# Top-k attention and two MoE layers on one core: half-chunk weight tiles, plain 32-bit scores for one batch, a guard on GpSimd, and new planner constants

## The chip, the cores and the metric

One Trainium2 chip, one core. The metric is the device time of one execution in microseconds; the time before is the median of three runs.

## The reference

Attention over 4 batches, 8 heads, 576 rows and a head size of 64. Of each row of scores only the 32 largest count; the rest are set to -1e9 ahead of the softmax. The attended rows, 2304 x 512, go through two dense layers (called MoE in the code):

```
scores = scale * q @ k.T;  kth = 32nd largest of the row
scores = where(scores >= kth, scores, -1e9)
attn   = exp(scores - max) / (sum + 1e-9);   x = attn @ v
x = (relu(x @ w_in) ** 2) @ w_out                    # 512 -> 2048 -> 512
x = max(x @ w1, x @ w2, x @ w3) @ w_out2             # 512 -> 768 -> 512
```

The weights come as 64-bit floats. All products must be good to about single precision.

## The kernel before, in words

The program is built by a planner that is part of it (class Plan, lines 85 to 243). Every operation is entered with its engine, a cost in ns (c_act, c_dve, c_pool and c_mm, lines 246 to 259), a priority, the buffers it reads and writes, and in some cases a slack: that many ns are added to the time at which the planner thinks it ready. Plan.run plays the program through once with these costs, hands out buffers by their number (nbufs, line 273), and so fixes the order in which each engine's instructions stand. On the chip each engine, and SP as the only queue that issues DMAs, then works through its list in that order and waits at each instruction for what it needs. Constants of the model: DBW, DL0, DL1 and DTR (line 35) are the DMA's bytes per ns, two latencies and the time of one transpose.

**Attention.** The work is cut into eight units (line 323): a batch's full 128-row tiles, three, one or three at a time, and a remainder of 64 rows of two heads. Each unit runs four times, once for each pair of heads p (attend, line 404). prep_k and prep_q (lines 354 and 390) load k and q already laid out, twice over in 128 partitions; ScalarE rounds all of it to the reduced 32-bit format of TensorE (lines 359 and 399), and GpSimd replaces it by the difference: in k for the lower 64 partitions, in q as a second plane. So one product over 128 partitions with the plane of high parts, and one with the plane of low parts, make the score (lines 494 to 504): two matmuls of 288 columns for each half of a score tile, four in the remainder. ScalarE scales them into s (line 429). Then VectorE takes the top 32 of 576 in four rounds of max (line 435) with three of match-replace between them (line 437); GpSimd makes a bias nb (line 439); ScalarE masks, takes exp and casts to 16 bits (lines 441 to 446); GpSimd makes the low 16-bit part; SP issues a DMA that transposes both parts (line 451); TensorE multiplies by v in nine small matmuls (line 462); ScalarE copies the result with its row sum into xs (line 465).

finish_x (line 506) divides by the row sum: VectorE adds a guard and doubles (line 508, slack 1000 ns), VectorE takes the reciprocal (line 510), GpSimd adds the two parts (line 515) and multiplies (line 516). TensorE transposes into x (lines 471, 486), ScalarE and VectorE split that into a high and a low part (lines 474, 476, 488, 490). There are 64 such divisions and 144 score tiles: 24, 12, 12 and 24 in the four units of the first two batches, and the same again.

**MoE.** Units 0; 1 and 2; 3; 4; 5 and 6; 7 feed six passes of 384 rows (moe, line 574). Each pass takes 28 weight chunks (8 of w_in, 8 of w_out, 9 of w1 to w3, 3 of w_out2), and each product is three matmuls: high x high, high x low, low x high (line 599). weights (line 535) brings a chunk as a tile wt of 2 x 1024 columns, four buffers. In the first pass a chunk is converted from 64-bit floats in two halves: SP loads the raw words into one of three slots (line 550), ScalarE forms the exponent part (line 557, through the helper line 308), VectorE shifts and merges (lines 559 and 561), ScalarE rounds to the high part (line 563), GpSimd subtracts for the low part (line 565, through the helper line 305), and SP stores the whole chunk to DRAM (line 567). The other five passes load chunks from there (line 540). A chunk's matmuls wait for the whole tile.

Of the kernel before, what the change touches and what calls it, by code (L numbers as in the profile page):

```python
# [23 lines left out]
D = 64  # L24
# [10 lines left out]
DBW, DL0, DL1, DTR = 360.0, 1280.0, 900.0, 1500.0  # L35
# [32 lines left out]
class Half:  # L68


    def __init__(self, bf, x):
        self.bf, self.x = bf, x

    def __getitem__(self, idx):
        return self.bf[(idx[0], self.x, *idx[1:])]

    def key(self, k):
        return self.bf, (self.x, k)
# [6 lines left out]
class Plan:  # L85
# [11 lines left out]
    def op(self, eng, ns, prio, reads, writes, fn, lat=0.0, slack=0.0):  # L97
        reads, writes = ([x[0].key(x[1]) if isinstance(x, tuple) and isinstance(x[0], Half) else x for x in y]
# [159 lines left out]
def c_mm(n):  # L258
    return max(n / 2.4 + 2.5, 107.0)
# [3 lines left out]
def kernel(ctx, tc, q, k, v, w_in, w_out, w1, w2, w3, w_out2, out):  # L263
# [9 lines left out]
    nbufs = {"ks": 1, "qs": 1, "vst": 2, "kt": 4, "qt": 1, "vt": 4, "vs": 1, "sm": 2, "sc": 2, "us": 6, "s": 6, "w": 2, "e": 3, "e16": 2,  # L273
             "et": 2, "mx": 4, "nb": 4, "rc": 4, "xs": 2, "xr": 2, "xg": 3, "xt": 3, "cv": 3,
             "hh": 6, "hl": 6, "r": 2, "m0": 1, "m1": 1, "ot": 2, "wt": 4,
# [64 lines left out]
    NRAW = 3  # L340
    wtile = buf("xt", [P, 2, KD, NW], F32R)
    work = [(wtile, x) for x in range(2 * KD * NW // 1024)]
    while len(work) < NRAW:
        t = const.tile([P, 2, KD, P], F32R, name=f"raw{len(work)}")
        work.append((keep(t), 0))
# [3 lines left out]
    kv = {}  # L349

# [39 lines left out]
    def prep_q(i, unit, p):  # L390
        b, tl, rem = unit[:3]
        w = len(tl) * 2 * P
        n = w + (3 * D if rem else 0)
        qs = buf("qs", [P, QW])
        ld(lambda: qs[:, 0:w], q[b, p, :, tl[0] * 2 * P:tl[0] * 2 * P + w], (qs, 0), P * w)
# [8 lines left out]
    def attend(i, unit, p):  # L404
# [10 lines left out]
        if g not in xt:  # L415
            t = buf("xt", [P, 2, KD, NW], F32R)
            xt[g] = Half(t, 0), Half(t, 1)
        xh, xl = xt[g]
        xg = buf("xg", [P, XW, P])
# [3 lines left out]
        for j, h in jobs:  # L423
            s = buf("s", [P, S])
            for f in range(2):
                ps = buf("b", [P, 512])
                cs = slice(f * HS, (f + 1) * HS)
                pe(A_S, c_mm(HS) * (2 if j >= 0 else 4), [kt, qt], [ps, (s, f)], scores(j, h, nt, qt, kt, ps, cs))
# [3 lines left out]
            for r in range(4):  # L432
# [3 lines left out]
                if r < 3:  # L436
                    dve(A_X, S, [src, (mx, r)], [w_], lambda src=src, mx=mx, m8=m8, w_=w_: nc.vector.match_replace(  # L437
                        out=w_[:], in_to_replace=mx[:, m8], in_values=src[:], imm_value=-3.0e38))
            gps(A_E, 1, [(mx, 0), (mx, 3)], [nb], lambda mx=mx, nb=nb: nc.gpsimd.tensor_scalar(  # L439
# [14 lines left out]
            for hh, c0, c1 in ([(0, 0, D), (1, D, P)] if j < 0 else [(h, 0, P)]):  # L454
# [9 lines left out]
                pe(A_E, 400.0, [et, vt], [ps, (xs, (max(j, 0) % 2, hh)), (xg, (j, hh))], av)  # L464
                act(A_X, VW, [ps], [(xs, (max(j, 0) % 2, hh))], lambda ps=ps, xs=xs, m=m, j=j, hh=hh: nc.scalar.copy(
                    xs[0:m, max(j, 0) % 2, hh, :], ps[0:m, 0:VW]))
            if j < 0:
# [19 lines left out]
        pe(A_S, 107.0 * nt, [xg], [ps, (xh, (p, col)), (xl, (p, col))], f)  # L487
        act(A_S, w, [ps, us], [(xh, (p, col))], lambda: nc.scalar.activation(
            xh[:, p, col:col + w], ps[:, 0:w], AF.Copy, scale=us[:]), ptr=1)
        dve(A_S, w, [ps, us, (xh, (p, col))], [(xl, (p, col))], lambda: nc.vector.scalar_tensor_tensor(  # L490
            xl[:, p, col:col + w], ps[:, 0:w], us[:], xh[:, p, col:col + w].bitcast(F32),
            op0=ALU.mult, op1=ALU.subtract), slack=SL / 2)

    def scores(j, h, nt, qt, kt, ps, cs):
        def run():
            if j >= 0:
                o = j * 2 * P + h * P
                seq = [(qt[:, x, o:o + P], kt[:, h, cs]) for x in range(2)]
# [34 lines left out]
    scratch = [keep(dr.tile([P, 2048], F32, name=f"wsc{n}")) for n in range(NCH)]  # L533

    def weights(g, n):
        src = chunk_src[n]
        a, f = src.shape[1], src.shape[2]
        wt = buf("wt", [P, 2, 1024], F32R)
        if g > 0:
            dma(W_, P * 8192, [scratch[n]], [wt], lambda: nc.sync.dma_start(  # L540
                wt[:].rearrange("p a b -> p (a b)").bitcast(F32), scratch[n][:]))
        else:
            for x in range(2):
                wk, off = raw = work[(2 * n + x) % len(work)]

                def part(u, wk=wk, off=off):
                    return wk[:].rearrange("p x a b -> p (x a b)").bitcast(U32)[
                        :, 1024 * off:1024 * off + 1024].rearrange("p (n u) -> p n u", u=2)[:, :, u]

                dma(W_, P * 4096, [], [raw], lambda x=x, wk=wk, off=off: nc.sync.dma_start(  # L550
                    wk[:].rearrange("p x a b -> p (x a b)").bitcast(U32)[
                        :, 1024 * off:1024 * off + 1024].rearrange("p (a f) -> p a f", f=f),
                    src[:, x * a // 2:(x + 1) * a // 2, :]))
                hi, lo = (wt, 2 * x), (wt, 2 * x + 1)
                cv = buf("cv", [P, 512], U32)
                words = lambda cv=cv: cv[:]
                act(C_M, 512, [raw], [cv], lambda part=part, cv=cv: prelu(
                    cv[:].bitcast(F32), part(1).bitcast(F32), -2.0 ** 32, scale=2.0 ** -112), psum=False)
                dve(C_D, 512, [cv], [cv], lambda cv=cv: nc.vector.tensor_scalar(  # L559
                    cv[:], cv[:], 3, None, op0=ALU.logical_shift_left), rate=0.5, slack=SL / 2)  # L560
                dve(C_D, 512, [raw, cv], [cv], lambda part=part, cv=cv: nc.vector.scalar_tensor_tensor(  # L561
                    cv[:], part(0), 29, cv[:], op0=ALU.logical_shift_right, op1=ALU.bitwise_or), rate=1.6)
# [193 lines left out]
```

## Time and profile before

| | us |
|---|---|
| median of 3 runs | 1109.63 (1108.77 to 1112.27) |
| profiled execution, its own time | 1109.87 |
| its span, first to last instruction | 1108.1 |
| mean granted TensorE clock in it | 0.912 |

| engine | busy us | share of the span |
|---|---|---|
| TensorE matmul | 962.6 | 87% |
| TensorE weight load | 892.5 | 81% |
| VectorE | 886.8 | 80% |
| ScalarE | 747.3 | 67% |
| GpSimd | 646.8 | 58% |

Busy time counts instructions in execution. A matmul's end is modelled, so the mean time of one matmul is longer than the distance from one to the next. A wait is put down to the engine and line that released it. In rows, PE is TensorE, PEld its weight loads, DVE VectorE, ACT ScalarE, POOL GpSimd, SP the queue that issues DMAs; L508 is line 508. "issue" is time in which an engine waited for nothing that the profile shows.

### The profile page before, as it was taken

The page shows a single profiled execution, that of the slowest core. Times are in us where ns is not written, and L with a number is a line of the kernel's source. Part 1 is how long each engine was busy: PE and PEld are TensorE (multiplying, and loading weights), DVE is VectorE, ACT ScalarE, POOL GpSimd, SP SyncE. Part 2 cuts the span into 40 slices and gives each one's busy share as a digit, 9 for nine tenths or more (in the row PEclk, how much of TensorE's full clock was granted, in tenths as well). Part 3 has the DMA queues.
Part 4 walks back from the last instruction along what each step waited for, and adds up shares of the span by engine and source line. Part 5 has one row for each costly group of instructions (what it writes and reads, how often), then busy time and mean ns, then how long its engine had stood idle before and what let it go on. Part 6 is the DMA issues. An engine that isn't in the chain of part 4 may idle for free.

```text
span 1108.1 us, 18444 instructions
## 1 busy us (share of the span) xinstructions
PE 962.6 (87%) x6116; PEld 892.5 (81%) x6116; DVE 886.8 (80%) x1856; ACT 747.3 (67%) x1572; POOL 646.8 (58%) x835
## 2 busy tenths in 40 slices
PE   3455527987878799999999999999999999999998
PEld 2344426876767689989899998899998999989997
DVE  7999999999999999899999999999999931100020
ACT  7776758887876777887888877978866753123321
POOL 5754568988887756665665768666655552112211
PEclk8556557998878899999999999999999999999999
DMA  8544595999899999999999999999999996776663
GB/s 290 138 93 68 119 300 142 311 261 285 275 287 303 279 328 325 270 293 277 291 265 271 278 280 265 251 273 251 247 273 267 268 279 248 249 257 254 262 243 140
DMA packets 221343, 278.56 MB, mean 251 GB/s; under 512 B 175680, under 2 KB 179776, under 8 KB 199744
## 3 DMA queue, kind: packets, MB, share of 16 engines
q1 hardware_dynamic: 221248, 277.39, 85.2%
q8 instruction: 48, 0.79, 0.3%
q14 instruction: 47, 0.39, 0.1%
HBM read 200.80 MB, written 34.08 MB: 212 GB/s over the span
## 4 chain that ended last, share of the span: by engine, by line
PE 49%; DVE 34%; DMA 6%; issue 4%; ACT 3%; POOL 3%; SPq 0%; POOLq 0%; ACTq 0%; DVEq 0%
PE a L599 32%; DVE mx L435 14%; DVE w L437 12%; PE b L599 10%; DMA et<-e 5%; PE b L503 3%; PE b L462 3%; DVE cv L561 3%; DVE cv L559 2%; DVE rc L508 1%; DMA xt<-in_moe_w_in_dram 1%; POOL hl L305 1%; POOL e L305 1%; PE b L486 0%; DVE m L650 0%
## 5 line engine op out<-in xcount | busy, mean ns | idle before, releaser
L435 DVE MAX8 mx<-w 128x8 f32<-128x576 f32 x432 | 312.0, 743 | 0.4
L305 POOL TENSOR_TENSOR e<-e,e 128x512 f16<-128x512 f32 (+1 forms) x288 | 215.1, 764 | 98.2 <-ACT e L446 64.8
L599 PE MATMUL a<-xt,wt 128*128 128x384 f32 x1296 | 249.8, 345 | 7.2 <-POOL wt L305 3.2
L599 PEld LDWEIGHTS a<-xt,wt 128*128 128x128 f32 x1296 | 228.6, 192 | 11.1 <-POOL wt L305 4.6
L599 PE MATMUL b<-xt,wt 128*128 128x384 f32 x1152 | 231.5, 344 | 0.4 <-DVE xt L490 0.4
L599 PE MATMUL a<-hh,wt 128*128 128x384 f32 x768 | 225.4, 346 | 0.1
L437 DVE MATCH_REPLACE8 w<-mx,w 128x576 f32<-128x576 f32 x288 | 212.1, 738 | 0.0
L599 PEld LDWEIGHTS b<-xt,wt 128*128 128x128 f32 x1152 | 203.4, 191 | 1.7 <-DVE xt L490 0.8
L503 PE MATMUL b<-kt,qt 128*128 128x288 f32 x640 | 139.0, 345 | 49.7 <-ACT s L429 16.4
L305 POOL TENSOR_TENSOR hl<-r,hh 128x384 fp32r<-128x384 f32 x96 | 99.5, 1036 | 140.8 <-ACT hh L625 133.8
L503 PEld LDWEIGHTS b<-kt,qt 128*128 128x128 f32 x640 | 114.5, 222 | 61.0 <-ACT s L429 20.4
L308 ACT ACTIVATE e<-s,mx 128x576 f32<-128x576 f32 x144 | 111.8, 778 | 58.4 <-DVE mx L435 49.9
L462 PEld LDWEIGHTS <-et 128*128 128x128 f16 (+1 forms) x1440 | 87.0, 110 | 75.7 <-DMA et<-e 45.3
L462 PE MATMUL b<-vt,et 128*128 128x129 f16 (+3 forms) x1440 | 103.2, 225 | 48.8 <-DMA et<-e 26.2
L599 PEld LDWEIGHTS a<-hh,wt 128*128 128x128 f32 x768 | 142.9, 190 | 1.0 <-ACT hh L625 0.4
L599 PE MATMUL a<-hl,wt 128*128 128x384 f32 x384 | 131.9, 344 | 11.6 <-POOL hl L305 11.4
L429 ACT ACTIVATE s<-b 128x288 f32<-128x288 f32 x288 | 107.3, 408 | 16.3 <-PE b L503 15.1
L443 ACT ACTIVATE e<-e,nb 128x576 f32<-128x576 f32 x144 | 111.7, 778 | 6.5 <-POOL nb L439 3.9
L435 DVE MAX8 mx<-s 128x8 f32<-128x576 f32 x144 | 106.2, 743 | 5.5 <-ACT e L308 5.5
L437 DVE MATCH_REPLACE8 w<-mx,s 128x576 f32<-128x576 f32 x144 | 106.2, 738 | 0.0
L446 ACT CAST e<-e 128x576 f16<-128x576 f32 x144 | 97.2, 676 | 10.1 <-DMA et<-e 9.7
L623 ACT ACTIVATE r<-b 128x384 f32<-128x384 f32 x96 | 46.9, 489 | 75.0 <-PE b L599 74.9
(60 smaller groups left out, 1257.4 us busy)
## 6 DMA issues: line engine op xcount, KB each, us to landing
wt<-wsc SPq DMA_DIRECT2D x140, 1024.0 KB, 5.5
wsc<-wt SPq DMA_DIRECT2D x28, 1024.0 KB, 5.9
xt<-in_moe_w_out_dram SPq DMA_DIRECT2D x22, 512.0 KB, 4.7
ks<-in_k_dram SPq DMA_DIRECT2D x16, 576.0 KB, 4.8
xt<-in_moe_w_dram SPq DMA_DIRECT2D x18, 512.0 KB, 4.8
xt<-in_moe_w_in_dram SPq DMA_DIRECT2D x16, 512.0 KB, 5.2
qs<-in_q_dram SPq DMA_DIRECT2D x16, 384.0 KB, 5.0
vst<-in_v_dram SPq DMA_DIRECT2D x16, 320.0 KB, 4.7
```

Of the source, the lines that this page charges most:

```text
L305: eng.tensor_tensor(out_ap, a, b, op=ALU.subtract)
L308: return nc.scalar.activation(out_ap, src, AF.Prelu, alpha=slope, **kw)
L429: act(A_S, HS, [ps], [(s, f)], lambda s=s, cs=cs, ps=ps: nc.scalar.activation(s[:, cs], ps[:, 0:HS], AF.Copy, scale=escale))
L435: dve(A_X, S, [src], [(mx, r)], lambda src=src, mx=mx, m8=m8: nc.vector.max(out=mx[:, m8], in_=src[:]))
L437: dve(A_X, S, [src, (mx, r)], [w_], lambda src=src, mx=mx, m8=m8, w_=w_: nc.vector.match_replace(out=w_[:], in_to_replace=mx[:, m8], in_va ...
L443: act(A_E, S, [e, nb], [e], lambda nb=nb, e=e: nc.scalar.activation(e[:], e[:], AF.Exp, bias=nb[:], scale=-1.0 / KEEP), psum=False, ptr=1)
L446: act(A_E, S, [e], [(e16, 0)], lambda e=e, e16=e16: nc.scalar.copy(e16[:, S:2 * S], e[:]), psum=False)
L462: nc.tensor.matmul(ps[0:m, 0:wv], et[:, mm_, c0:c1], vt[:, hh, vc, 0:wv], start=x == 0, stop=x == 8)
L503: nc.tensor.matmul(ps[:, 0:HS], a, c, start=m == 0, stop=m == len(seq) - 1)
L561: dve(C_D, 512, [raw, cv], [cv], lambda part=part, cv=cv: nc.vector.scalar_tensor_tensor(cv[:], part(0), 29, cv[:], op0=ALU.logical_shift_ ...
L599: nc.tensor.matmul(o, x, y, start=first and i == 0 and m == 0, stop=last and i == n - 1 and m == 2)
L623: act(MA, N, [ps], [r], lambda r=r, ps=ps: nc.scalar.activation(r[:, 0:N], ps[:, 0:N], AF.Relu))
```

## The change

The tile wt becomes half a chunk (2 x 512 columns, eight buffers); each half has its own load, conversion, store and place in DRAM, and a matmul waits for the half that it reads. The buffer cv of the conversion goes; it uses the output tile ot, of which there are now three. Batch 0's k and q are loaded once into 64 partitions of kt and qt, without a cast or a subtraction, and its scores are single products of 32-bit operands. The guard of line 508 moves to GpSimd, and neither it nor the reciprocal has slack. nbufs gives more e16, et, mx and nb buffers. The planner's costs change: DMA bytes per ns, the transpose, a matmul, match-replace, nb. An x tile's dependencies are kept for each pair p by a class Slot, with the same buffer behind it. Units, priorities and the three raw slots stay.

```diff
-DBW, DL0, DL1, DTR = 360.0, 1280.0, 900.0, 1500.0
+DBW, DL0, DL1, DTR = 390.0, 1280.0, 900.0, 2300.0
 def c_mm(n):
-    return max(n / 2.4 + 2.5, 107.0)
+    return max(n / 2.4 + 13.0, 107.0)
-    nbufs = {... "e16": 2, "et": 2, "mx": 4, "nb": 4, ... "xt": 3, "cv": 3, ... "ot": 2, "wt": 4,
+    nbufs = {... "e16": 3, "et": 3, "mx": 8, "nb": 8, ... "xt": 3, ... "ot": 3, "wt": 8,
+    PLAIN = (0,)
     def prep_k(b, p):
+        if b in PLAIN:
+            kt = buf("kt", [P, 2, S], F32R)
+            ld(lambda: kt[0:D].rearrange("p h s -> p (h s)").bitcast(F32), k[b, p, 0:D, :], kt, D * 2 * S)
+            return kt
...
+        if b in PLAIN:
+            qt = buf("qt", [P, 2, QW], F32R)
+            if tl:
+                ld(lambda: qt[0:D, 0, 0:w].bitcast(F32), q[b, p, 0:D, ...], (qt, 0), D * w)
+            if rem:
+                ld(lambda: qt[0:D, 0, w:n].bitcast(F32), q[b, p, 0:D, 8 * P:8 * P + 3 * D], (qt, 1), D * 3 * D)
+            return qt
...
-                pe(A_S, c_mm(HS) * (2 if j >= 0 else 4), [kt, qt], [ps, (s, f)], scores(j, h, nt, qt, kt, ps, cs))
+                pe(A_S, (4 * HS / 2.4 if b in PLAIN else 2 * c_mm(HS)) * (1 if j >= 0 else 2), [kt, qt], [ps, (s, f)],
+                   scores(j, h, nt, qt, kt, ps, cs, b in PLAIN))
...
-                    dve(A_X, S, [src, (mx, r)], [w_], ... match_replace(
+                    dve(A_X, S + 50, [src, (mx, r)], [w_], ... match_replace(
-            gps(A_E, 1, [(mx, 0), (mx, 3)], [nb], ...
+            gps(A_E, 110, [(mx, 0), (mx, 3)], [nb], ...
...
+            xs = range(1 if plain else 2)
+            if plain:
+                seq = [(a[0:D].bitcast(F32), c[0:D].bitcast(F32)) for a, c in seq]
...
-        dve(A_S, 4, [xs], [rc], lambda: nc.vector.tensor_scalar(
-            rc[0:pn, 0:nt], xs[0:pn, 0:nt, :, 0:1], eguard, 2.0, op0=ALU.add, op1=ALU.mult), slack=SL)
+        gps(A_S, 100, [xs], [rc], lambda: nc.gpsimd.tensor_scalar(
+            rc[0:pn, 0:nt], xs[0:pn, 0:nt, :, 0:1], eguard, 2.0, op0=ALU.add, op1=ALU.mult))
         dve(A_S, 4, [rc], [rc], lambda: nc.vector.reciprocal(rc[0:pn, 0:nt], rc[0:pn, 0:nt]))
...
+        h = a // 2
+        wts = [half_chunk(g, n, x, src[:, x * h:(x + 1) * h, :], f) for x in range(2)]
+        def view(r, kk):
+            return wts[kk // h][:, r].rearrange("p (a f) -> p a f", f=f // 2)[:, kk % h]
+        return (lambda kk: wts[kk // h]), view
+    def half_chunk(g, n, x, src, f):
+        wt, dst = buf("wt", [P, 2, 512], F32R), scratch[n][x]
+        if g > 0:
+            dma(W_, P * 4096, [dst], [wt], lambda: nc.sync.dma_start(
+                wt[:].rearrange("p a b -> p (a b)").bitcast(F32), dst[:]))
+            return wt
+        raw = work[(2 * n + x) % len(work)]
+        cv = buf("ot", [P, 512])
...
+        dma(W_, P * 4096, [wt], [dst], lambda: nc.sync.dma_start(
+            dst[:], wt[:].rearrange("p a b -> p (a b)").bitcast(F32)))
...
-                group(ps, KD, lambda i, wi=wi: [wi, *xkeys(i)],
+                group(ps, KD, lambda i, wi=wi: [wi(i), *xkeys(i)],
```

## Rows read from the trace of the kernel before

**Rows 1.** The page's 40 slices of the span: busy tenths of TensorE and VectorE

```profile
PE   3455527987878799999999999999999999999998
...
DVE  7999999999999999899999999999999931100020
```

**Rows 2.** Windows: length; PE, PEld, DVE, ACT, POOL busy; clock, DMA share, GB/s

```profile
0.00:176.00 176.00, 80.14 (x427) 64.52 (x427) 168.19 (x352) 120.89 (x245) 106.33 (x140) 0.60 0.62 167
176.00:386.00 210.00, 171.10 (x1039) 152.18 (x1039) 206.70 (x404) 166.44 (x356) 173.62 (x189) 0.88 0.91 273
386.00:1108.00 722.00, 711.37 (x4654) 675.79 (x4652) 511.95 (x1103) 460.02 (x973) 366.87 (x508) 1.00 0.90 266
```

**Rows 3.** The chain of waits by line, 0 to 386 us

```profile
by line: DVE mx L435 29.8%; DVE w L437 24.7%; DVE cv L561 8.1%; issue 7.8%; DVE cv L559 6.0%; PE a L599 4.0%; DMA xt<-in_moe_w_in_dram 3.1%; DVE rc L508 3.0%; DVE m L650 1.2%; POOL wt L305 1.0%; DVE xt L490 1.0%; POOL hl L305 0.9%; ACT cv L
```

**Rows 4.** TensorE's waits from 386 us on, the largest sum: us, times, longest

```profile
PE a L599 <- POOL hl L305: 3.1, 6, 0.6
```

**Rows 5.** Lines 508 and 510: min/median/max ns; then line 508 by windows (VectorE busy)

```profile
L508 DVE TENSOR_SCALAR rc<-xs x64: 140/330/2443, 49.8 to 913.5; 128x2 f32<-128x2 f32 x32, 128x4 f32<-128x4 f32 x16, 64x2 f32<-64x2 f32 x16
...
L510 DVE RECIPROCAL rc<-rc x64: 133/147/178, 50.8 to 913.7; 128x2 f32<-128x2 f32 x32, 128x4 f32<-128x4 f32 x16, 64x2 f32<-64x2 f32 x16
...
0.00:176.00 176.00, 3.88 (x9) 0.60 0.62 167
176.00:386.00 210.00, 10.08 (x15) 0.88 0.91 273
```

**Rows 6.** Groups by line, whole span: busy us, mean ns | idle before, releaser

```profile
L377 DVE TENSOR_SCALAR us<-sc 128x1 uint32<-128x1 uint32 x16 | 2.2, 139 | 2.0 <-ACT sc L375 1.9
...
L439 POOL TENSOR_SCALAR nb<-mx 128x1 f32<-128x1 f32 x144 | 46.5, 323 | 60.9 <-DVE mx L435 48.4 <-DVE us L377 1.7 <-DVE rc L510 1.3
...
L305 POOL TENSOR_TENSOR e<-e,e 128x512 f16<-128x512 f32 x144 | 172.0, 1194 | 98.2 <-ACT e L446 64.8 <-issue 26.8 <-DVE mx L435 1.6
```

**Rows 7.** Waits up to 386 us: VectorE's second largest; TensorE's for weight tiles

```profile
DVE rc L508 <- ACT xs L465: 0.9, 1, 0.9
...
PE a L599 <- POOL wt L305: 5.7, 5, 2.5
PE a L599 <- ACT wt L563: 5.7, 3, 3.0
```

**Rows 8.** GpSimd's subtraction for k, group by line, 0 to 176 us

```profile
L305 POOL TENSOR_TENSOR kt<-ks,kt 64x1152 fp32r<-64x1152 f32 x7 | 18.5, 2636 | 9.3 <-ACT kt L359 7.0 <-issue 2.0
```

**Rows 9.** The start on VectorE, timeline: start us, us, what [idle before]

```profile
7.44 1.33 DVE L559 TENSOR_SCALAR cv<-cv 128x512 uint32<-128x512 uint32 x1 [7.44 <-ACT cv L308]
...
8.80 2.18 DVE L561 SCALAR_TENSOR_TENSOR cv<-xt,cv 128x512 uint32<-128x512 uint32 x1
...
14.11 1.41 DVE L435 MAX8 mx<-s 128x8 f32<-128x576 f32 x2
```

**Rows 10.** The conversion on VectorE: min/median/max ns, first and last start

```profile
L559 DVE TENSOR_SCALAR cv<-cv x56: 399/461/1485, 7.4 to 385.0; 128x512 uint32<-128x512 uint32 x56
...
L561 DVE SCALAR_TENSOR_TENSOR cv<-xt,cv x56: 659/751/2447, 8.8 to 386.0; 128x512 uint32<-128x512 uint32 x56
```

**Rows 11.** Score matmuls: a timeline row, line 503 by window (PE, PEld), line 374

```profile
253.02 1.23 PE L503 MATMUL b<-kt,qt 128*128 128x288 f32 x8
...
0.00:176.00 176.00, 50.85 (x152) 36.78 (x152) 0.60 0.62 167
...
L374 PE MATMUL b<-sm,ones x32: 165/250/373, 17.0 to 711.7; 128*128 128x1 f32 x32
```

**Rows 12.** SP's queue: line 540's issue, min/median/max ns; line 550's wait in us

```profile
L540 SPq DMA_DIRECT2D wt<-wsc x140: 319/325/1120, 384.9 to 1087.6; - x140
...
SPq L550 <- DVE cv L561: 63.4, 33, 4.7
```

**Rows 13.** Line 435, the max operations, by windows: VectorE busy (count)

```profile
0.00:176.00 176.00, 83.69 (x119) 0.60 0.62 167
176.00:386.00 210.00, 70.90 (x98) 0.88 0.91 273
```

More of the change, by code (lines that the diff above doesn't have):

```diff
@@ L65, in open, with __init__ @@
             self.tile = self.pool.tile(self.shape, self.dtype, tag=t, name=t)
[L68 to L72 removed]
+class Slot:
+    def __init__(self, bf, x, p):
+        self.bf, self.x, self.p = bf, x, p
     def __getitem__(self, idx):
[L75 removed]
+        return self.bf[(idx[0], self.x, self.p, *idx[1:])]
     def key(self, k):
[L78 removed]
+        return self.bf, (self.x, self.p, k)
 class Op:
@@ L97, in op @@
     def op(self, eng, ns, prio, reads, writes, fn, lat=0.0, slack=0.0):
-        reads, writes = ([x[0].key(x[1]) if isinstance(x, tuple) and isinstance(x[0], Half) else x for x in y]
+        reads, writes = ([x[0].key(x[1]) if isinstance(x, tuple) and isinstance(x[0], Slot) else x for x in y]
                          for y in (reads, writes))
@@ L339 @@
     QW = max(len(u[1]) * 2 * P + (3 * D if u[2] else 0) for u in units)
[L340 to L345, printed above, removed]
+    spare = buf("xt", [P, 2, KD, NW], F32R)
+    work = [(spare, x) for x in range(2 * KD * NW // 1024)]
     xt = {}
     kv = {}
+    PLAIN = (0,)
     def ld(dst, s, bf, n):
@@ L414, in attend @@
         kt, vt, us = kv[b, p]
-        if g not in xt:
+        if (g, p) not in xt:
             t = buf("xt", [P, 2, KD, NW], F32R)
-            xt[g] = Half(t, 0), Half(t, 1)
-        xh, xl = xt[g]
-        xg = buf("xg", [P, XW, P])
+            xt.update({(g, d): (Slot(t, 0, d), Slot(t, 1, d)) for d in range(KD)})
+        xh, xl = xt[g, p]
+        xg = buf("xg", [P, XW, P]) if tl else None
         xs = None
@@ L480, in attend @@
                 finish_x(xs, P, j + 1 - j0, xg, lambda j0=j0, j=j: xg[:, j0:j + 1, :])
+        if not tl:
+            return
         w = nt * P
@@ L532 @@
     NCH = len(chunk_src)
-    scratch = [keep(dr.tile([P, 2048], F32, name=f"wsc{n}")) for n in range(NCH)]
+    scratch = [[keep(dr.tile([P, 1024], F32, name=f"wsc{n}_{x}")) for x in range(2)] for n in range(NCH)]
     def weights(g, n):
@@ L537, in weights @@
         a, f = src.shape[1], src.shape[2]
-        wt = buf("wt", [P, 2, 1024], F32R)
-        if g > 0:
[L540 to L562, printed above, removed]
-                act(C_A, 512, [cv], [hi], lambda x=x, words=words: nc.scalar.copy(
-                    wt[:, 0, 512 * x:512 * x + 512], words().bitcast(F32)), psum=False)
-                gps(C_P, 512, [cv, hi], [lo], lambda x=x, words=words: sub(
-                    nc.gpsimd, wt[:, 1, 512 * x:512 * x + 512], words().bitcast(F32), wt[:, 0, 512 * x:512 * x + 512].bitcast(F32)))
-            dma(W_, P * 8192, [wt], [scratch[n]], lambda: nc.sync.dma_start(
-                scratch[n][:], wt[:].rearrange("p a b -> p (a b)").bitcast(F32)))
@@ L574, in moe @@
     def moe(g):
         N = width[g]
-        xh, xl = xt[g]
+        xs = [xt[g, p] for p in range(KD)]
         c3 = 3 * c_mm(N)
@@ L579, in moe, with xv @@
         cn = [0]
-        def xcols(d):
-            return [(d, u[4]) for u in units if u[3] == g] + [(d, "r")]
+        xcols = [u[4] for u in units if u[3] == g and u[1]] + ["r"]
         def xkeys(d):
-            return [(x, kx) for x in (xh, xl) for kx in xcols(d)]
+            return [(x, kx) for x in xs[d] for kx in xcols]
+        def xv(d):
+            return xs[d][0][:, 0:N], xs[d][1][:, 0:N]
         def nextw():
```

82 lines of the change are left out of this document (48 added, 34 removed).

## The prediction, made before the changed kernel was run

> **What bounds the kernel now.** I read the slices of the page first. VectorE is full from the first slice to the 31st and nearly idle after that; TensorE is half idle at the left and full from about the fifteenth slice to the end [rows 1]. So two engines bound the run one after the other, and the question is where the one takes over. The windows answer it. Up to 176 us VectorE is busy for 168.2 us and TensorE for 80.1, at a granted clock of 0.60; from 176 to 386 us VectorE for 206.7 of 210 us and TensorE for 171.1, at 0.88; from 386 us on TensorE has 711.4 of 722 us at the full clock [rows 2]. The chain says the same: up to 386 us it runs through the top-k and the weight conversion on VectorE [rows 3]. I chose 386 us because the last conversion on VectorE stands there [rows 10], and behind it TensorE's wait lists are all but empty: the largest sum is 3.1 us [rows 4], and none of it is for a weight tile. What follows: time saved behind 386 us anywhere but in TensorE's own work buys nothing, and time saved on VectorE ahead of 386 us pulls the start of TensorE's full stretch, and with it the end, forward.
>
> The sum is made against the profiled execution, 1109.87 us with a span of 1108.1; it lies 0.24 us above the median of 1109.63. About 0.3% (3.3 us) is what a measurement of this kernel can tell from no change.
>
> **Row-sum guard to GpSimd.** Line 508 stands 64 times on VectorE, for two or four elements, and yet its median is 330 ns and its longest 2443 ns, while the reciprocal behind it, on as many elements, never takes more than 178 ns [rows 5]. Up to 386 us there are 9 + 15 = 24 of them with 3.88 + 10.08 = 13.96 us on the bounding engine. That goes: **-14.0 us**. The other 40 lie where TensorE bounds, and are worth nothing. What comes instead: 64 short operations on GpSimd, priced by the 323 ns of line 439's operation on one column [rows 6]: 24 x 0.323 = 8 us ahead of 386 us, on an engine that has 106 + 174 = 280 of 386 us busy [rows 2]; beside other work, so nothing. The reciprocal now waits for GpSimd, without the 1000 ns of slack that the guard had in the plan, and behind it in VectorE's order stand the next max and match-replace operations. The trace has no such wait. The nearest row without slack is line 377, which waits 2.0 us in 16 instances, 0.125 us each [rows 6]; at the other end, the reciprocal waits out one whole 512-column operation of GpSimd (1.19 us) [rows 6] and the guard's own 0.32, about 1.5 us. I take 0.125, since VectorE is the late engine in this stretch and hardly ever waits (bar the start, 0.9 us at most for one line [rows 7]): 24 x 0.125 = **+3.0 us** (0 to +36).
>
> **Batch 0 without high and low part.** The casts of lines 359 and 399 on ScalarE and the subtractions on GpSimd go for four k and eight q tiles; of GpSimd's, k alone has 4 x 2.64 = 10.5 us [rows 8]. So the first score comes sooner. But VectorE is not idle there: from 7.44 us it converts weights until the first max at 14.11 us [rows 9], and that work stays. What it gains is that two of these conversions take 1.33 and 2.18 us beside the k subtraction, against 0.40 and 0.66 at the shortest [rows 9, 10]: 0.93 + 1.52 = **-2.4 us** (0 to -4). Later on, less GpSimd work up to 176 us and more (15 guards) from 176 to 386 us, where 45 of the 56 conversions are, about cancel: 0 (-2 to +2).
>
> The products themselves: a half of a score tile takes two reduced products of 288 columns, eight of which take 1.23 us at the full clock [rows 11], so 0.154 us each. Afterwards it takes one 32-bit product. The only true 32-bit product of the trace is line 374, 16 calls that stand as 32 records [rows 11], so two records to a call: at the low end a plain product costs what the pair cost, 0; at the high end each record takes twice as long, as it would at the lower of the two clocks, 1.2 against 2.4 GHz: 2 x 0.154 = 0.308 us more. Batch 0 has 80 such calls (48 in its first unit, 32 in the second), so 0 to 24.6 us. I cost it at nothing either way: 152 of the 160 reduced products that they replace run before 176 us, where TensorE has 96 us free [rows 2, 11]. If that cover is gone, the 32 calls of the second unit fall into the first MoE pass, for 9.9 us. The Trainium skill ("FP8 and Floating Point Precision", TensorE Precision Notes) speaks against this edit: it gives a true 32-bit product as four passes through the array. By it the high end is the price, by the row's two records the low end; as long as the cover holds, the sum is the same by both, and the difference is taken up as a rival below. No row here shows four passes.
>
> **Half-chunk weight tiles.** A matmul of the first pass now waits for the half that it reads, not for the whole chunk. Up to 386 us TensorE waits 5.7 us for the high and 5.7 us for the low part of a weight tile [rows 7]. I take half of it: **-5.7 us** (0 to -11.4). On SP's queue there are 140 more loads and 28 more stores, at 325 ns to issue [rows 12], 54.6 us over the run, of which the 28 stores, 9.1 us, lie ahead of 386 us. The queue is in order, so raw loads and transposes stand behind them; but the raw loads wait there for 63.4 us anyway until line 561 has freed their slot [rows 12], and later TensorE's waits for transposes and weights are below 3.1 us [rows 4]: 0. If that cover is gone, the 9.1 us are the price.
>
> **Refitted planner and deeper buffers.** This moves order alone. VectorE has no wait ahead of 386 us that one more mx, nb, e16 or et buffer would take away [rows 7], so 0 for these. For the order the ends are: TensorE has 39 us not busy between 176 and 386 us and a clock of 0.88, so some 39 + 0.12 x 171 = 60 us that a perfect order could win back; and as much to lose. Of the 60, the terms above take 19. I take 0 for the order, since no row prices it.
>
> Sum: -14.0 + 3.0 - 2.4 - 5.7 = -19.1; 1109.87 - 19.1 = 1090.8, say **1091 us**. I put the case's own range at 1080 to 1100.
>
> **Rivals.** *B, the order wins more.* By 386 us VectorE has done (119 + 98) / 4 = 54 score tiles' top-k [rows 13], while the second MoE pass needs 48 (24 + 12 + 12 of the first three units), and TensorE stands idle for weights meanwhile; if the new costs put conversions ahead of these 6 tiles, the first pass ends earlier. For it: the 60 us above. Against: the conversions wait for three raw slots [rows 12], which the change leaves as they are. The 6 tiles are worth, with 70.90 / 98 = 0.72 us for a max and as much for each of the three match-replaces, 6 x 7 x 0.72 = 30 us of VectorE [rows 13]; I take 26 of them: -45, 1065 us.
>
> *C, the gain is eaten in place.* The plain products cost the high end, fall into the first MoE pass and run at the lower clock: 32 x 2 x 0.308 = 20 us, against my 19: 1091 + 20 = 1111 us, no change. For it: TensorE's clock is at 0.60 up to 176 us [rows 2] and the first pass will start sooner. Against: the free time. The same comes out if the stalls of line 508 only move on to the next VectorE operation.
>
> *D, slower: the reciprocal's wait takes the place of the guard.* GpSimd takes its operations in order; if a guard stands behind a 512-column difference, VectorE, which everything waits for, stands still with it. At the 1.5 us above, 24 x 1.5 = 36 in place of 3: 1091 + 33 = 1124 us. It decides from (19.1 + 3.0 + 3.3) / 24 = 1.06 us per reciprocal on. For it: the slack that was there is gone, and GpSimd has 174 of 210 us busy [rows 2]. Against: VectorE is the late one, so GpSimd should have the guard done.
>
> **How the numbers follow.** My case 0.48, B 0.23, C 0.10, D 0.14, and 0.05 for an order that loses, which also lies on the slow side. Faster by over 0.3% is mine and B, 0.71; the same is C, 0.10; slower 0.19. The range runs from just below B to between C and D: below 1060 I leave 0.09, above 1116 0.11.
>
> **What would show it.** In the profile after: line 510 without a stall and VectorE's busy time some 34 us less; the first max before 14 us; 160 or 320 records of line 503 up to 250 us; the last conversion near 367 us, not 386 [rows 10]; TensorE full from there on. Wrong if the reciprocals are long or idle gaps stand before them, if TensorE waits for weights behind 400 us, or if the end moves while the last conversion does not.

## The result, and the profile after

The changed kernel takes 1100.19 us (median of four runs, 1099.21 to 1100.86); the kernel before took 1110.95 beside it. The ratio is 0.9898, with a 95% interval of 0.9881 to 0.9916: 10.8 us or 1.0% faster, by 8 to 9 us less than forecast. The profiled execution has a span of 1097.4 us, 10.7 less than before.

The page of the changed kernel, busy times and slices, answers to [rows 1]:

```profile
PE 997.0 (91%) x6116; PEld 898.0 (82%) x6116; DVE 860.7 (78%) x1792; ACT 746.2 (68%) x1560; POOL 635.9 (58%) x887
...
PE   6677759898778799999999999999999999999998
...
DVE  5999999999999999999999999999999501100020
...
PEclk9999999998998999999999999999999999999999
```

The shape is the same: VectorE full first, TensorE full afterwards. (The full clock in the first six slices is not what TensorE ran at; see the last section.) To see where one takes over I take the end of the first MoE pass, the end of its last output matmul. Windows of the kernel before, up to that point and from it to the end (length; TensorE, its weight loads, VectorE, ScalarE, GpSimd busy; clock, DMA share, GB/s):

```profile
0.00:395.20 395.20, 260.44 (x1512) 224.41 (x1513) 384.09 (x772) 292.66 (x609) 288.51 (x334) 0.75 0.78 227
...
395.20:1108.10 712.90, 702.17 (x4605) 668.08 (x4603) 502.75 (x1085) 454.69 (x963) 358.31 (x502) 1.00 0.90 265
```

The same of the changed kernel:

```profile
0.00:387.50 387.50, 297.37 (x1512) 230.65 (x1513) 372.03 (x742) 288.25 (x597) 268.36 (x347) 0.96 0.80 224
...
387.50:1097.40 709.90, 699.60 (x4605) 667.39 (x4604) 488.66 (x1051) 457.95 (x964) 367.56 (x541) 1.00 0.95 267
```

By this point 1512 matmuls are done in both, and 4605 are left. The front is 7.7 us shorter, the rest 3.0. In the front VectorE has 384.09 - 372.03 = 12.1 us less work, but its idle time grew from 11.1 to 15.5 us: 12.1 - 4.4 = 7.7. VectorE is busy for 96 to 97% of this front in both kernels, TensorE for 66% before and 77% after, so that VectorE is the late engine here, as foreseen, and its groups tell where the 12.1 come from. VectorE of the kernel before up to 395.2 us, groups by line (count | busy us, mean ns | idle before, releaser):

```profile
L561 DVE SCALAR_TENSOR_TENSOR cv<-xt,cv 128x512 uint32<-128x512 uint32 x56 | 57.1, 1022 | 0.1
L559 DVE TENSOR_SCALAR cv<-cv 128x512 uint32<-128x512 uint32 x56 | 37.2, 668 | 8.5 <-ACT cv L308 7.7 <-POOL nb L439 0.8
...
L508 DVE TENSOR_SCALAR rc<-xs 128x2 f32<-128x2 f32 (+2 forms) x25 | 15.0, 599 | 0.9 <-ACT xs L465 0.9
...
L510 DVE RECIPROCAL rc<-rc 128x2 f32<-128x2 f32 (+2 forms) x25 | 3.7, 147 | 0.0
```

The same of the changed kernel up to 387.4 us (lines 445, 579, 581, 525 and 378 are 435, 559, 561, 510 and 377 of before):

```profile
L445 DVE MAX8 mx<-w 128x8 f32<-128x576 f32 x165 | 119.6, 744 | 0.0
...
L581 DVE SCALAR_TENSOR_TENSOR ot<-xt,ot 128x512 uint32<-128x512 uint32 x56 | 55.0, 983 | 0.0
L579 DVE TENSOR_SCALAR ot<-ot 128x512 uint32<-128x512 uint32 x56 | 42.9, 768 | 0.1
L445 DVE MAX8 mx<-s 128x8 f32<-128x576 f32 x56 | 41.3, 741 | 8.4 <-ACT s L439 8.4
...
L525 DVE RECIPROCAL rc<-rc 128x2 f32<-128x2 f32 (+2 forms) x25 | 3.8, 150 | 2.5 <-POOL rc L523 2.4
...
L378 DVE TENSOR_SCALAR us<-sc 128x1 uint32<-128x1 uint32 x9 | 1.3, 140 | 4.0 <-ACT sc L376 4.0
```

The 15.0 us of the guard are gone. The 56 conversions together (shift and merge) went from 57.1 + 37.2 = 94.3 to 97.9 us, 3.6 more, although they are as many and of the same shape. The idle time is 8.4 us ahead of the first max, 4.0 behind it and 2.4 ahead of reciprocals.

The last conversion, by which I had placed the end of this stage, moved less than the end of the pass, answer to [rows 10]:

```profile
L581 DVE SCALAR_TENSOR_TENSOR ot<-xt,ot x56: 662/877/2340, 10.1 to 382.5; 128x512 uint32<-128x512 uint32 x56
```

It starts 3.5 us earlier than before, at 382.5 us. So about half of the front's 7.7 us lies behind it, where TensorE works off what is left of the first pass.

The guard and the reciprocal, lines 523 and 525 of the changed kernel (min/median/max ns), answer to [rows 5]:

```profile
L523 POOL TENSOR_SCALAR rc<-xs x64: 182/195/631, 46.1 to 903.3; 128x2 f32<-128x2 f32 x32, 128x4 f32<-128x4 f32 x16, 64x2 f32<-64x2 f32 x16
...
L525 DVE RECIPROCAL rc<-rc x64: 134/155/180, 47.0 to 903.5; 128x2 f32<-128x2 f32 x32, 128x4 f32<-128x4 f32 x16, 64x2 f32<-64x2 f32 x16
```

On GpSimd the guard has a median of 195 ns and none takes longer than 631 ns; the reciprocal never takes more than 180 ns, much as before.

The start on VectorE, timeline of the changed kernel, answers to [rows 9]:

```profile
8.40 0.76 DVE L445 MAX8 mx<-s 128x8 f32<-128x576 f32 x1 [8.40 <-ACT s L439]
9.08 0.41 DVE L579 TENSOR_SCALAR ot<-ot 128x512 uint32<-128x512 uint32 x1
...
10.13 0.68 DVE L581 SCALAR_TENSOR_TENSOR ot<-xt,ot 128x512 uint32<-128x512 uint32 x1
...
18.28 0.15 DVE L378 TENSOR_SCALAR us<-sc 128x1 uint32<-128x1 uint32 x1 [4.01 <-ACT sc L376]
```

and on TensorE:

```profile
5.67 11.85 PE L518 MATMUL b<-kt,qt 64*128 64x288 f32 x24 [5.67 <-DMA qt<-in_q_dram]
17.45 0.58 PE L375 MATMUL b<-sm,ones 128*128 128x1 f32 x2
```

The first max stands at 8.40 us, not at 14.11. The two conversions that took 1.33 and 2.18 us there now take 0.41 and 0.68. But line 375, a one-column product for the scale of v, stands behind 24 records of plain products that take 11.8 us, and line 378 waits for it: 4.0 us on VectorE. Together it sat idle 8.4 + 4.0 = 12.4 us at the start, against 7.44 before [rows 9]. The same two instructions of the kernel before:

```profile
17.02 0.28 PE L374 MATMUL b<-sm,ones 128*128 128x1 f32 x2
...
21.84 0.15 DVE L377 TENSOR_SCALAR us<-sc 128x1 uint32<-128x1 uint32 x1
```

The product started at nearly the same time there, behind 24 records of reduced products. But VectorE came to line 377 only at 21.84 us and did not wait. So it takes both, a product that is no earlier and a place earlier in VectorE's order.

TensorE's waits of the changed kernel up to 387.5 us, those for weight tiles (us in total, times, longest), answer to [rows 7]:

```profile
PE a L616 <- POOL wt L305: 15.4, 14, 3.7
...
PE a L616 <- ACT wt L583: 2.4, 4, 0.8
...
PE b L616 <- POOL wt L305: 1.1, 1, 1.1
PE b L616 <- ACT wt L583: 0.9, 1, 0.9
```

20 waits with 19.8 us, where there were 8 with 11.4. From 387.5 us on the longest sum is 4.4 us, for a low part (3.1 before [rows 4]).

### The profile page after: what moved, and what is told of

It is laid out like the page before. It is cut to its first block, busy times and chain, and to the rows that moved or that the text cites. A ratio compares the mean times of both kernels' runs of the same rounds, so it can differ in the third digit from the quotient of the medians.

```text
span 1097.4 us, 18750 instructions
## 1 busy us (share of the span) xinstructions
PE 997.0 (91%) x6116; PEld 898.0 (82%) x6116; DVE 860.7 (78%) x1792; ACT 746.2 (68%) x1560; POOL 635.9 (58%) x887
## 4 chain that ended last, share of the span: by engine, by line
PE 60%; DVE 24%; POOL 7%; issue 6%; ACT 3%; DMA 0%; SPq 0%; POOLq 0%; ACTq 0%; DVEq 0%
PE a L616 37%; PE b L616 13%; DVE mx L445 10%; DVE w L447 8%; PE b L518 5%; PE b L472 4%; DVE ot L581 3%; POOL e L305 2%; POOL hl L305 2%; DVE ot L579 2%; POOL wt L305 1%; PE b L498 1%; POOL kt L305 0%; ACT e L308 0%; DMA qt<-in_q_dram 0%
## 5 line engine op out<-in xcount | busy, mean ns | idle before, releaser
L305 POOL TENSOR_TENSOR e<-e,e 128x512 f16<-128x512 f32 (+1 forms) x288 | 217.8, 769 | 92.9 <-ACT e L456 77.1
L616 PE MATMUL b<-xt,wt 128*128 128x384 f32 x1152 | 235.7, 346 | 4.0 <-DVE xt L502 1.8
L616 PE MATMUL a<-hh,wt 128*128 128x384 f32 x768 | 222.2, 342 | 1.1 <-ACT hh L642 1.0
L518 PE MATMUL b<-kt,qt 128*128 128x288 f32 (+1 forms) x640 | 170.8, 400 | 25.8 <-DMA qt<-in_q_dram 8.5
L518 PEld LDWEIGHTS b<-kt,qt 128*128 128x128 f32 (+1 forms) x640 | 121.2, 222 | 49.1 <-ACT xs L475 12.6
L472 PEld LDWEIGHTS <-et 128*128 128x128 f16 (+1 forms) x1440 | 84.3, 108 | 58.2 <-DMA et<-e 31.8
L472 PE MATMUL b<-vt,et 128*128 128x129 f16 (+3 forms) x1440 | 101.4, 223 | 24.2 <-DMA et<-e 11.8
L445 DVE MAX8 mx<-s 128x8 f32<-128x576 f32 x144 | 107.0, 745 | 10.8 <-ACT s L439 10.7
```

Of the source, the lines that this page charges most:

```text
L305: eng.tensor_tensor(out_ap, a, b, op=ALU.subtract)
L445: dve(A_X, S, [src], [(mx, r)], lambda src=src, mx=mx, m8=m8: nc.vector.max(out=mx[:, m8], in_=src[:]))
L472: nc.tensor.matmul(ps[0:m, 0:wv], et[:, mm_, c0:c1], vt[:, hh, vc, 0:wv], start=x == 0, stop=x == 8)
L518: nc.tensor.matmul(ps[:, 0:HS], a, c, start=m == 0, stop=m == len(seq) - 1)
L616: nc.tensor.matmul(o, x, y, start=first and i == 0 and m == 0, stop=last and i == n - 1 and m == 2)
```

## The experiments

Four to twelve runs were timed of each kernel, beside the kernel before on the same chip. "End of pass" is the end of the first MoE pass in the profile, "rest" the time from there to the end. Front and rest of the changed kernel are 387.5 and 709.9, of the kernel before 395.2 and 712.9. Where the order is new, the work that is done by the end of the pass is not quite the same (1508 to 1529 matmuls).

| kernel | median us | before beside it | ratio (95%) | end of pass | rest |
|---|---|---|---|---|---|
| a_guard_dve | 1112.11 | 1111.07 | 1.0014 (1.0006 to 1.0023) | 405.4 | 704.4 |
| a_noplain | 1118.18 | 1111.07 | 1.0066 (1.0053 to 1.0079) | 406.6 | 710.2 |
| a_dither | 1109.92 | 1111.07 | 0.9989 (0.9978 to 1.0000) | 398.8 | 711.3 |
| a_oldcost | 1105.16 | 1111.07 | 0.9945 (0.9925 to 0.9965) | 392.0 | 710.9 |
| b_guard_pool | 1127.98 | 1110.88 | 1.0146 (1.0127 to 1.0165) | 408.9 | 718.4 |
| b_dither | 1117.68 | 1110.88 | 1.0065 (1.0040 to 1.0090) | 393.7 | 719.6 |
| half_only | 1120.61 | 1110.88 | 1.0087 (1.0069 to 1.0105) | 401.7 | 716.0 |
| b_newcost | 1125.39 | 1110.88 | 1.0132 (1.0114 to 1.0150) | 413.2 | 709.1 |
| fa_guard_dve | 1110.18 | 1111.44 | 0.9985 (0.9972 to 0.9999) | 392.9 | 713.2 |
| fb_guard_pool | 1109.84 | 1111.44 | 0.9974 (0.9959 to 0.9989) | 394.1 | 714.0 |
| fb_guard_act | 1105.22 | 1111.44 | 0.9945 (0.9928 to 0.9961) | 391.5 | 712.6 |
| fa_guard_act | 1101.32 | 1111.44 | 0.9903 (0.9883 to 0.9923) | 388.7 | 711.3 |

Names with a_ and fa_ start from the changed kernel, those with b_ and fb_ from the kernel before; half_only is the changed kernel with its other parts taken back. The first eight are planned anew, so each edit also moves the order of everything; the last four keep the order fixed.

**Parts taken out of the changed kernel, or put alone into the kernel before.**

a_guard_dve, the guard back on VectorE:

```diff
-        gps(A_S, 100, [xs], [rc], lambda: nc.gpsimd.tensor_scalar(
+        dve(A_S, 4, [xs], [rc], lambda: nc.vector.tensor_scalar(
...
+            ..., slack=SL)
```

> The changed kernel with the guard back on VectorE, with its slack of 1000 ns; all else as changed. My theory: the guard's time on VectorE ahead of the end of the first MoE pass (15.0 us for 25 of them in the kernel before) is what the change gained; with it back the time is 10 to 15 us longer, 1110 to 1115 us, and the guard's line shows again a median over 300 ns and a longest over 2 us. Rival, the gain is the planner's order: within 4 us of the changed kernel, 1096 to 1104 us.

b_guard_pool, the guard on GpSimd in the kernel before:

```diff
-        dve(A_S, 4, [xs], [rc], lambda: nc.vector.tensor_scalar(
+        gps(A_S, 100, [xs], [rc], lambda: nc.gpsimd.tensor_scalar(
```

> The kernel before with the guard alone moved to GpSimd, without slack, as in the change. My theory: the 15.0 us of VectorE ahead of the end of the first MoE pass go, some 3 us come back as waits of the reciprocal: 8 to 14 us shorter than before, 1097 to 1103 us. Rival, the reciprocal's wait takes the guard's place, or the stalls move on to the next VectorE operation: within 3 us of before, 1107 to 1114 us.

Back on VectorE, the guard costs the whole gain: 1112.11 us. Alone on GpSimd it does not bring the gain but loses 17 us. The two contradict each other if the guard is all that an edit moves, so something else moves with it.

half_only, half-chunk tiles with the old costs, guard, products and other buffers (the dependencies of the x tiles by pair stay in it; the lines are shown against the kernel before):

```diff
-             ... "xt": 3, "cv": 3, ... "ot": 2, "wt": 4,
+             ... "xt": 3, ... "ot": 3, "wt": 8,
+    PLAIN = ()
```

> The kernel before with the half-chunk weight tiles alone (halves of wt in eight buffers, cv from the output tiles); guard, scores, other buffers and planner's costs as before. My theory by the forecast: 0 to 11 us shorter, most likely 6, so 1105 us; by the trace of the changed kernel, where TensorE waits longer for weight tiles than before (19.8 us against 11.4 up to the end of the first pass), nothing: 1108 to 1114 us. Rival, twice the DMA issues cost: over 1114 us.

10 us slower than before. Its waits of TensorE for weight tiles up to the end of the first pass:

```profile
PE a L616 <- POOL wt L305: 13.1, 16, 2.2
...
PE a L616 <- ACT wt L583: 9.9, 7, 3.3
...
PE b L616 <- POOL wt L305: 1.2, 2, 0.7
```

These are 24.2 us in 25 waits. The same sum is 19.8 to 26.6 us in all eight kernels with half tiles, the changed one included, and 10.5 to 13.0 in the six with whole ones, whatever their order. So half tiles did not shorten these waits but about doubled them. What that costs in time isn't shown, since TensorE is not the late engine there.

b_newcost, the kernel before with the new costs:

```diff
-DBW, DL0, DL1, DTR = 360.0, 1280.0, 900.0, 1500.0
+DBW, DL0, DL1, DTR = 390.0, 1280.0, 900.0, 2300.0
-    return max(n / 2.4 + 2.5, 107.0)
+    return max(n / 2.4 + 13.0, 107.0)
...
```

> The kernel before with the planner's costs of the change alone (DMA bytes per ns, transpose, matmul, match-replace, nb). My theory: order alone, within 4 us of before, 1107 to 1115 us. Rival, the refit carries the gain: 8 to 12 us shorter, 1099 to 1103 us.

a_oldcost, the changed kernel with the costs of before (the same lines the other way):

> The changed kernel with the planner's costs of before (DMA bytes per ns, transpose, matmul, match-replace, nb); tiles, buffers, plain scores and the guard's place as changed. My theory: the costs move order alone and are worth little: within 4 us, 1096 to 1104 us. Rival, the refit is the gain: 8 to 12 us longer, 1108 to 1112 us.

The new costs lose 14.5 us in one kernel and gain 5 in the other. They are no better as such.

a_noplain, the changed kernel with high and low part for batch 0 too:

```diff
-    PLAIN = (0,)
+    PLAIN = ()
```

> The changed kernel with batch 0 treated like the others (high and low part again). My theory: plain products cost the start, since VectorE sat idle 12.4 us there against 7.7 before and TensorE's products took twice as long; without them the time is 3 to 6 us shorter, 1094 to 1097 us. Rival, the GpSimd work that they save (about 22 us up to 176 us) is worth more than the start: 3 to 8 us longer, 1103 to 1108 us.

18 us slower than the changed kernel: the theory had the wrong sign, and the rival was too small. VectorE up to the end of the first pass, groups by line:

```profile
L581 DVE SCALAR_TENSOR_TENSOR ot<-xt,ot 128x512 uint32<-128x512 uint32 x56 | 61.9, 1110 | 0.1
L579 DVE TENSOR_SCALAR ot<-ot 128x512 uint32<-128x512 uint32 x56 | 44.1, 792 | 9.0 <-ACT ot L308 9.0
```

The conversions take 61.9 + 44.1 = 106.0 us, 8.1 more than in the changed kernel, while GpSimd has 293.0 us of work in that stage against 268.4. That fits a gain of the plain products by way of less GpSimd work beside VectorE, which I had put at about nothing but for the start. The order moved too, though: in a_dither, below, the conversions take 102.8 us beside 267.6 us of GpSimd work, as much as in the changed kernel, so that a new order alone lengthens them by 4.9 us. So it isn't shown.

**Order alone.** a_dither, the changed kernel with one cost of the planner 1 ns less:

```diff
-    return max(n / 2.4 + 13.0, 107.0)
+    return max(n / 2.4 + 12.0, 107.0)
```

> The changed kernel with one number of the planner's model moved by 1 ns (a matmul's fixed cost 12 in place of 13 ns): the same instructions in a slightly other order. It measures how much of any difference is order. My theory, the gain has causes that an order does not undo: within 3 us, 1097 to 1103 us. Rival, the gain is an accident of one order: further off than 5 us, most likely back to 1105 to 1112 us.

b_dither, the kernel before with the same cost 1 ns more:

```diff
-    return max(n / 2.4 + 2.5, 107.0)
+    return max(n / 2.4 + 3.5, 107.0)
```

> The kernel before with one number of the planner's model moved by 1 ns (a matmul's fixed cost 3.5 in place of 2.5 ns): the same instructions in a slightly other order, to see how much of any difference is order. My theory: within 3 us of before, 1108 to 1114 us. Rival, the order's accidents are as large as the change's gain: further off than 5 us.

Nothing but the order differs, and the times move by 9.7 us (ratio to the changed kernel 0.9989 / 0.9898 = 1.009) and 6.8 us: as much as the whole change brings. The window of a_dither to the end of its first pass:

```profile
0.00:398.80 398.80, 301.61 (x1512) 235.31 (x1512) 377.84 (x742) 288.62 (x597) 267.58 (x348) 0.94 0.78 218
```

VectorE and TensorE have executed as many instructions as in the changed kernel up to its end (742 and 1512), 11.3 us later: 5.8 us of VectorE busy and 5.5 us idle. In b_dither the loss lies elsewhere: its first pass ends 1.5 us earlier than in the kernel before, and the rest takes 6.7 us longer. Both edits, the only two of their kind, moved the time by 7 to 10 us; so differences of 5 to 18 us among the re-planned kernels can't be put down to what their edits do by their times alone.

**The guard with the order fixed.** Here the planner keeps its entry for the guard, and only the instruction goes to another engine. TensorE's and SP's instructions stand in the same order, those of the other engines too but for the 64 guards.

fa_guard_dve, the changed kernel's order, guard on VectorE:

```diff
-        gps(A_S, 100, [xs], [rc], lambda: nc.gpsimd.tensor_scalar(
+        gps(A_S, 100, [xs], [rc], lambda: nc.vector.tensor_scalar(
```

> The changed kernel with the guard emitted on VectorE, but planned as if it were on GpSimd, so that all other instructions keep their places. Theory 1: 8 to 13 us longer than the changed kernel, 1108 to 1113 us. Theory 2: within 3 us of it, 1097 to 1103 us.

Against the changed kernel 0.9985 / 0.9898 = 1.009, or 9.6 us by the ratios. Its groups on VectorE up to 392.9 us:

```profile
L581 DVE SCALAR_TENSOR_TENSOR ot<-xt,ot 128x512 uint32<-128x512 uint32 x56 | 55.2, 988 | 0.0
L579 DVE TENSOR_SCALAR ot<-ot 128x512 uint32<-128x512 uint32 x56 | 41.4, 740 | 0.1
...
L523 DVE TENSOR_SCALAR rc<-xs 128x2 f32<-128x2 f32 (+2 forms) x25 | 10.4, 416 | 0.0
```

The guard takes 10.4 us, the conversions 96.6, 1.3 less than in the changed kernel. The front is 5.4 us longer, the rest 3.3; what lengthens the rest isn't shown. With the guard on VectorE, all else that was changed is worth only 1 to 2 us in this order (ratio 0.9985 to the kernel before).

fb_guard_pool, the order of the kernel before, guard on GpSimd:

```diff
-        dve(A_S, 4, [xs], [rc], lambda: nc.vector.tensor_scalar(
+        dve(A_S, 4, [xs], [rc], lambda: nc.gpsimd.tensor_scalar(
```

> The kernel before with the guard on GpSimd, but planned as if it were still on VectorE: every other instruction of every engine keeps its place, and the guard stands in GpSimd's order at its old planned time. Theory 1, the guard's stall on VectorE is a real cost and the new order ate the gain in the run that moved it through the planner: 8 to 13 us shorter than before, 1098 to 1103 us. Theory 2, the stall moves on to the conversion's operations on VectorE (lines 559 and 561): VectorE's busy time up to the end of the first pass falls by less than 5 us, and the time is within 3 us of before, 1107 to 1114 us.

Only 2.9 us by the ratio (1.2 to 4.6). Its groups up to 394.1 us:

```profile
L561 DVE SCALAR_TENSOR_TENSOR cv<-xt,cv 128x512 uint32<-128x512 uint32 x56 | 59.8, 1070 | 0.1
...
L559 DVE TENSOR_SCALAR cv<-cv 128x512 uint32<-128x512 uint32 x56 | 41.2, 740 | 9.1 <-ACT cv L308 9.1
...
L510 DVE RECIPROCAL rc<-rc 128x2 f32<-128x2 f32 (+2 forms) x25 | 3.9, 157 | 3.4 <-POOL rc L508 3.2
```

15.0 us of guard are gone, but the 56 conversions take 101.0 us instead of 94.3, and 3.4 us of waits stand ahead of the reciprocals. VectorE's busy time falls by 384.1 - 378.4 = 5.7 us, its idle time rises by 4.7, and the pass ends 1.1 us earlier; the span of this profiled execution, 1108.1 us, is that of the kernel before. The longest guard shows where a stall can go. Timeline of the kernel before:

```profile
340.06 2.44 DVE L508 TENSOR_SCALAR rc<-xs 128x2 f32<-128x2 f32 x1
342.42 0.41 DVE L559 TENSOR_SCALAR cv<-cv 128x512 uint32<-128x512 uint32 x1
```

The same place with the guard on GpSimd:

```profile
341.01 2.74 DVE L559 TENSOR_SCALAR cv<-cv 128x512 uint32<-128x512 uint32 x1
```

The conversion that stood behind the guard now takes 2.74 us, what the two took together.

Is that because GpSimd has 64 operations more? fb_guard_act, the same order, guard on ScalarE:

```diff
-        dve(A_S, 4, [xs], [rc], lambda: nc.vector.tensor_scalar(
-            rc[0:pn, 0:nt], xs[0:pn, 0:nt, :, 0:1], eguard, 2.0, op0=ALU.add, op1=ALU.mult), slack=SL)
+        dve(A_S, 4, [xs], [rc], lambda: nc.scalar.activation(
+            rc[0:pn, 0:nt], xs[0:pn, 0:nt, :, 0:1], AF.Copy, scale=2.0, bias=2.0 * eguard), slack=SL)
```

> The kernel before with the guard on ScalarE (2 x + 2 guard in one activation), in the same fixed order. ScalarE has copied the row sum itself, and it adds no GpSimd work. Theory 1: as with GpSimd or up to 4 us better, 1095 to 1102 us. Theory 2, stalls of VectorE's conversions come from GpSimd's operations: without 64 more of them the conversions do not lengthen, so also shorter here, 1095 to 1102 us, but clearly better than with GpSimd.

Groups up to 391.5 us:

```profile
L561 DVE SCALAR_TENSOR_TENSOR cv<-xt,cv 128x512 uint32<-128x512 uint32 x56 | 59.9, 1072 | 0.1
...
L559 DVE TENSOR_SCALAR cv<-cv 128x512 uint32<-128x512 uint32 x56 | 40.8, 733 | 9.3 <-ACT cv L308 9.3
```

The conversions take 100.7 us, as long as with the guard on GpSimd; the one behind the longest guard takes 2.73 us here too. So it is not the added operations of GpSimd that lengthen them. For that one the stall has moved on from the guard; the rest of the 6.4 to 6.7 us is spread over other conversions, some longer and some shorter, and that it is the same stall is argued, not shown. The gain is 6.1 us by the ratio, less than both theories had.

fa_guard_act, the order of the changed kernel, guard on ScalarE (the same edit at line 523):

> The changed kernel with the guard on ScalarE in place of GpSimd, in the changed kernel's fixed order. Theory 1: within 3 us of the changed kernel, 1097 to 1103 us, since 64 short GpSimd operations cost it little. Theory 2: 3 to 6 us shorter, 1094 to 1097 us, with shorter conversions on VectorE. Rival: ScalarE stands at the guard for xs where GpSimd had time, and the time is longer than 1103 us.

1101.32 us, the changed kernel's time within 0.1%. None of the twelve is faster than the changed kernel.

## Why the prediction was right or wrong

**What bounds the kernel: right in the main.** VectorE is the late engine up to the end of the first pass, and TensorE is full behind it. But what TensorE then needs is not constant: 709.9 us in the changed kernel and 712.9 before, and 704.4 to 719.6 over all kernels. And the mark was a poor one. I had named as a sign of being wrong that the end moves while the last conversion does not: forecast near 367 us, it moved from 386.0 to 382.5, while the span fell by 10.7; in b_dither it stayed (385.9) and the time rose by 6.8. VectorE's busy time fell by 26.1 us in the whole run, not by 34.

The direction held, and of the forecast 19.1 us, 10.8 came. The time lies 0.2 us outside the case's own range of 1080 to 1100 and inside the wide one of 1060 to 1116. That the time fell at all is in part luck: with one cost of the planner 1 ns less, the same change measures 0.9989, as good as no gain (a_dither).

**Guard, -14.0: the mechanism is shown, its size hangs on the order.** With the order fixed the guard's place is worth 9.6 us in the changed kernel, and 2.9 us (on GpSimd) or 6.1 (on ScalarE) in the kernel before. The step that failed is "That goes: -14.0 us": I took the whole busy time of line 508 as saved. The operation's own part is small (25 at its shortest, 0.140 us [rows 5], are 3.5 us); the rest of its 15.0 us is stall. In fb_guard_pool the conversions took 6.7 us more and the reciprocals' waits 3.4, which left 5 of the 15.0, and the pass ended 1.1 us earlier. That is the last sentence of rival C, which I had priced in full or not at all; it happened in part.

**Reciprocal's wait, +3.0: right.** 2.4 us up to 387.4 us in the changed kernel, 3.2 in fb_guard_pool. Rival D is out.

**Start, -2.4: wrong sign.** The first max did come before 14 us and the two conversions got short, but VectorE sat idle 12.4 us in place of 7.44. I left out that VectorE, which takes its work in order, comes to the v-scale sooner now, while the plain products, longer on TensorE, keep the v-scale product where it was, at 17 us.

**Plain products at nothing on TensorE: right but for the start, and the price is the high end.** 160 records of the plain form stand for the 80 calls. At the full clock, timeline of the changed kernel on TensorE:

```profile
188.16 2.20 PE L518 MATMUL b<-kt,qt 64*128 64x288 f32 x8
190.30 0.59 PE L472 MATMUL b<-vt,et 128*128 128x129 f16 x9
```

Eight records in 190.30 - 188.16 = 2.14 us, 0.267 each and 0.535 a call. The pair of reduced products is 0.267: the eight of [rows 11] begin at 253.02 us, and the next instruction of the kernel before at 254.09:

```profile
254.09 1.75 PE L599 MATMUL b<-xt,wt 128*128 128x384 f32 x9
```

(My 0.154 us for one came from 1.23 us, which counts the modelled end of the last; by the distance it is 0.134.) A 32-bit product so costs twice the pair. The Trainium skill ("FP8 and Floating Point Precision", TensorE Precision Notes) gives a true 32-bit product as four passes through the array; 0.535 is four times the 0.134 of one reduced product, and the trace agrees. Of the free time there was enough otherwise: the pass ends earlier, though TensorE is busy for 297.4 us of the front and not 260.4.

**Half-chunk tiles, -5.7: failed.** "I take half of it" was wrong in sign: 19.8 us of waits for weight tiles, in 20 pieces, where 11.4 in 8 stood. The experiments bear out the sign: 19.8 to 26.6 us with half tiles, 10.5 to 13.0 with whole ones. A reading: TensorE waits as long as VectorE is late with the conversions; a smaller tile releases it sooner for a shorter stretch, and then it waits for the next. That is argued, not shown. The time of half_only, 10 us slower, is within what order alone can do.

**Order, 0: the size was not in the sum.** I kept ends of -60 and +60 and took 0, "since no row prices it". The two 1-ns edits price it: 7 to 10 us. It is the largest uncertainty of all. Rival B is out: VectorE has done (165 + 56) / 4 = 55.2 score tiles' top-k by the end of the pass, not 48.

**The sum.** In the front: guard -15.0, conversions +3.6, top-k (0.3 tiles less) and the rest -0.7, idle +4.4: -7.7. Of the 3.0 us after it, 2.6 stand in TensorE's busy time (702.17 and 699.60 us for the same 4605 matmuls) and 0.4 in its waits; why the same matmuls take less isn't shown.

In the order that was run, the guard's place accounts for 9.6 of the 10.8 us. What plain products, half tiles and costs are worth each stays open, since each of those edits moves the order.

## What to carry to other kernels

When a tiny operation shows a long busy time, look at its shortest instance: that much is its own work; the rest is stall, and some of it can turn up in the next operations of the same engine. Where a planner fixes the order, first measure what a meaningless 1-ns edit of a cost does; a part smaller than that can only be judged with the order held fixed, by moving the instruction and leaving its entry in the plan. A product that gets longer delays what stands behind it in its queue, even where that engine has time to spare. And that an engine's busy and idle time add up to a stage says nothing about what bounds it; a mark such as the last conversion should move with the end in the experiments too, before a sum is built on it.

## What the runs showed of the hardware that was not expected

The granted clock of the changed kernel's profile reads 1.00 up to 181 us, against 0.60 up to 176 us before [rows 2]. For most of that stretch it is not a rise. Nine small matmuls of line 472, timeline of the changed kernel:

```profile
141.18 0.98 PE L472 MATMUL b<-vt,et 128*128 128x129 f16 x9
...
168.62 0.98 PE L472 MATMUL b<-vt,et 128*128 128x129 f16 x9
```

The same group took 0.94 us in the kernel before at 37.41 us, where the granted clock was 0.50, and 0.59 us at 190.30 us in the changed one, where it is 1.00:

```profile
37.41 0.94 PE L462 MATMUL b<-vt,et 128*128 128x129 f16 x9 [0.26 <-DMA et<-e]
```

So at 141 and 169 us TensorE ran at the lower of its two levels, 1.2 GHz, where the profile shows a granted clock of 1.00. A clock of 1.00 should be held against the time of a known group of matmuls.

The loads of kt into 64 partitions land later than larger ones into 128. DMA issues of the changed kernel (count, KB each, median us to landing):

```profile
ks<-in_k_dram SPq DMA_DIRECT2D x12, 576.0 KB, 4.9
...
kt<-in_k_dram SPq DMA_DIRECT2D x4, 288.0 KB, 9.2
```

The partitions are not the reason. All four kt loads are issued in the first 6 us, among the raw loads. The first of them, issued before 1 us, lands fast, and a ks load into 128 partitions that is issued behind the four, at 6.7 us, takes 11.1 us:

```profile
kt<-in_k_dram SPq DMA_DIRECT2D x1, 288.0 KB, 3.8
...
ks<-in_k_dram SPq DMA_DIRECT2D x1, 576.0 KB, 11.1
```

So the 9.2 us go with the place of these loads in the run, behind the other loads of the start.
